# Placing VectorE work and tanh by a clock model at emission, dense item ahead of P·V, and an explicit order of dense items, in a fused attention and MLP kernel

## The chip, the cores and the metric

One NeuronCore of a Trainium2 chip. The metric is the device time of one execution in microseconds, on that core. Every time below is of a fast run; where two kernels are compared, the ratio is the mean time of one kernel's fast runs over the mean time of the other's fast runs of the same rounds, on the same chip, so it is not quite the ratio of the medians that are quoted beside it. The groups differ a little (the kernel before had medians of 1120.8 to 1123.9 us in the five groups of runs, two of them on one chip and two on another), so ratios are the numbers to compare across groups.

## The reference

`x` is 2048 tokens of 1024 features, bf16. The result is `x + attention(xn) * silu(mlp(xn))`, with 32 heads of 32 and an MLP width of 3584.

```python
xn = layernorm(x)
qkv = xn @ wqkv                                   # 32 heads, Dh = 32
p = softmax(q @ k.T * Dh**-0.5); s = (p @ v) @ wo
y = layernorm(xn)
h = gelu_tanh(y @ w1 + b1)                        # 2048 x 3584
g = silu(h @ w2 + b2)
out = x + s * g
```

## The kernel before

The program is emitted by Python into one instruction list per engine, with semaphores worked out from the tiles that each operation reads and writes. So the order of emission is the order in which each engine runs.

Attention is 512 *units*: 8 groups of 4 heads, 8 blocks of 256 queries, 8 blocks of 256 keys. In a unit PE computes scores S for four heads, row-tiled, into four PSUM banks; ACT does two exponentials of 128x1024; PE then does P·V and the row sums, column-tiled, into the one accumulator bank. PE is filled up with one *dense item* per unit, column-tiled, into the one remaining bank (bank 7): W1 (168 items), W2 (48 items cut into 3 or 4 parts), Q/K projections (84), V projections (48), the output projection WO (48). The tokens of the MLP go in six chunks, five of 352 and a last one of 288. Units 0 to 7 overlap the prologue (layer norm, first Q, K, V).

A finished dense item is evicted by VectorE. For W1 a chain follows on VectorE: add bias and evict, square, cube; then one tanh on ACT for two items; then two "gates" `(1+tanh)*x` on VectorE. After eight units VectorE also evicts the accumulator and scales it.

```python
def later(cost, fn, lag=1, first=False):          # queue a VectorE operation
    dq.append((cur["u"] + lag, cost, fn))         # not before unit u + lag
def run_dq(budget, limit=None): ...               # emit queued operations up to a budget in us

# W1, after its matmuls ...
def cube():
    op("vector", ...)
    if cubes[m2] == 2:
        act_tasks[cur["u"] + 1].append(tanh)      # tanh: in the next unit
def tanh():
    op("scalar", ... ACT.Tanh ...)
    for i, (xq, kq, fq) in enumerate(pairs[m2]):
        later(0.45, lambda ...: gate(i, xq, kq, fq), lag=0, first=soon)
...
while u < NU + 2 or ...:                          # the unit loop
    s_unit(u)                                     # PE: scores
    for t in act_tasks.pop(u, ()): t()            # ACT: tanh
    exp_unit(u)                                   # ACT: two exponentials
    if 2 <= u < NU + 2: pv_unit(u - 2)            # PE: P.V of two units ago
    for s in it.steps[lo:hi]: s(state["bank"])    # PE: dense item
    room = BUDGET - (0.8 if ended else 0.0)       # BUDGET = 1.35 us
    room -= run_dq(room)                          # VectorE: what is queued ...
    if hi == len(it.steps): it.finish(...)        # ... and then the eviction
```

The order of the dense items came from a loop with ratios and credits (W1 and projections mixed, then the W2 items of the chunk, and so on).

The softmax here doesn't subtract the row's maximum and nothing guards it: scores larger than these inputs give would overflow.

## Time and profile before

| | before |
|---|---|
| time, median of 3 | 1121.26 us (1120.38 to 1122.04) |
| span of the profiled run | 1120.0 us |
| first scores / unit 8 / last scores start at | 18.8 / 59.3 / 1098.9 us |

The page of the kernel before: the busy time of each engine with its share of the span, and the chain of work that ended last, followed backwards.

```profile
span 1120.0 us, 63277 instructions
...
PE 1085.4 (97%) x29952; PEld 692.4 (62%) x29952; DVE 621.5 (55%) x1415; ACT 1053.0 (94%) x1197; POOL 24.0 (2%) x64
...
PE 52%; ACT 43%; DVE 2%; DMA 1%; issue 1%; SPq 1%; DVEq 0%
ACT P L745 38%; PE ps L314 31%; PE ps L733 8%; PE ps L762 8%; PE ps L765 5%; ACT u L478 4%; DMA wq<-in_A_wqkv_dram 1%; DVE hT L484 1%; ACT thz L520 0%; PE ps L305 0%; SPq L223 0%; ACT xnT L308 0%; DMA xnT<-gT_scratch 0%; DVE xb L461 0%; DVE
```

PE is busy 97% of the time and ACT 94%, and the chain goes back and forth between them. Neither is simply "the" bottleneck, so the reading has to go to single units. This is the timeline of one unit with a Q item (columns: start us, duration us, engine, line, operation, out<-in, shapes, count, and in brackets the idle time of the engine before it with what ended it).

```profile
501.36 0.40 PE L733 MATMUL ps<-QT,KT 32*128 32x256 bf16 x8
...
501.69 0.29 PE L762 MATMUL ps<-P,VP 128*32 128x256 bf16 x4
...
502.14 1.37 PE L314 MATMUL ps<-xnT,wq 128*32 128x352 bf16 x32
...
503.44 0.40 PE L733 MATMUL ps<-QT,KT 32*128 32x256 bf16 x8
503.56 0.52 DVE L336 CAST QT<-ps 128x352 bf16<-128x352 f32 x1 [1.44 <-PE ps L314]
```

Read the starts, not the durations, since matmuls overlap: S to P·V 0.33 us, P·V to dense 0.45, dense to the next S 1.30. The Trainium skill, "TensorE: Matmul & The Clock Gate", section "Back-to-back issue gap", gives N/2.4 + 2.5 ns from one isolated matmul with N columns to the next. The trace agrees: 8 rounds of four column-tiled matmuls with N=352 are 8 x 149.2 = 1193 ns, and what is left of 1300 is about 107 ns for passing from column-tiled to row-tiled matmuls. S to P·V is 2 x 109.2 + 109 in the same way. So a W1 or Q unit takes PE 2.07 us when nothing disturbs it, a V unit 1.75. On ACT, exponentials start every 0.90 to 0.92 us, so a unit takes it about 1.83, and a W1 unit 0.34 more for its half of a tanh (0.68 us from the start of a tanh to the next start).

With these undisturbed times one can count *stalls* in the whole trace: for each stretch of S, P·V or dense matmuls, the time from its start to the start of the next, less rounds x (N/2.4 + 2.5) and less the passage (106 to 109 ns between S and the others, 10 between P·V and dense). I do this from unit 8 to unit 511. It gives 26.6 us for the kernel before: 15.2 ahead of S (PE waits for an exponential to free score banks), 6.4 ahead of a dense item (PE waits for VectorE to evict bank 7), and 5.1 as pauses *inside* runs of matmuls that wait for nothing.

What a stall ahead of a dense item looks like, in the timeline of the kernel before:

```profile
955.05 1.21 PE L314 MATMUL ps<-yTc,war 128*32 128x288 bf16 x32
...
956.19 0.40 PE L733 MATMUL ps<-QT,KT 32*128 32x256 bf16 x8
...
956.72 0.82 ACT L478 ACTIVATE u<-u 128x576 f32<-128x576 f32 x1
...
957.57 1.20 DVE L484 SCALAR_TENSOR_TENSOR hT<-u,xb 128x288 bf16<-128x288 f32 x3 [1.75 <-ACT u L478]
958.87 0.52 DVE L461 TENSOR_SCALAR xb<-ps,b1T 128x288 f32<-128x288 f32 x1
...
959.44 1.38 PE L314 MATMUL ps<-xnT,wq 128*32 128x352 bf16 x32 [2.30 <-DVE xb L461]
```

The W1 item that starts at 955.05 is done at about 956.3. Its eviction (L461) starts at 958.87 only: three gates (L484) stand ahead of it, and the first of them waited 1.75 us for a tanh (L478). PE is idle for 2.30 us before the next dense item. The waits by total time (who, for whom: us, times, longest) show that VectorE often stands like this, but charge PE little:

```profile
PEld ps L733 <- ACT P L745: 86.6, 260, 1.9
...
DVE gst L524 <- ACT thz L520: 32.1, 19, 2.2
...
DVE hT L484 <- ACT u L478: 13.5, 26, 1.7
PE ps L733 <- ACT P L745: 9.8, 29, 1.7
...
PEld ps L314 <- DVE xb L461: 4.7, 8, 2.6
...
PE ps L314 <- DVE xb L461: 2.7, 2, 2.3
```

The chain of waits in the stretch from 896 to 1000 us, which holds the last, 288-wide chunk. There a W1 unit takes PE only 1.86 us but ACT 1.83 + 0.29:

```profile
by line: ACT P L745 81.3%; ACT u L478 7.1%; issue 3.3%; PE ps L314 2.8%; DVE hT L484 1.2%; PE ps L733 1.1%; ACT thz L520 0.9%; SPq L413 0.9%; DVE xb L461 0.5%; DVE gst L524 0.5%; SPq L527 0.3%; PE ps L762 0.3%; PE ps L765 0.2%; DVEq L110 0.
```

89% of that stretch is ACT work on the chain (81.3, 7.1 and 0.9), so PE is the one that waits.

### The profile page before, as it was taken

The page shows a single profiled execution, that of the slowest core. Times are in us where ns is not written, and L with a number is a line of the kernel's source. Part 1 is how long each engine was busy: PE and PEld are TensorE (multiplying, and loading weights), DVE is VectorE, ACT ScalarE, POOL GpSimd, SP SyncE. Part 2 cuts the span into 40 slices and gives each one's busy share as a digit, 9 for nine tenths or more (in the row PEclk, how much of TensorE's full clock was granted, in tenths as well). Part 3 has the DMA queues.
Part 4 walks back from the last instruction along what each step waited for, and adds up shares of the span by engine and source line. Part 5 has one row for each costly group of instructions (what it writes and reads, how often), then busy time and mean ns, then how long its engine had stood idle before and what let it go on. Part 6 is the DMA issues. An engine that isn't in the chain of part 4 may idle for free.

```text
span 1120.0 us, 63277 instructions
## 1 busy us (share of the span) xinstructions
PE 1085.4 (97%) x29952; PEld 692.4 (62%) x29952; DVE 621.5 (55%) x1415; ACT 1053.0 (94%) x1197; POOL 24.0 (2%) x64
## 2 busy tenths in 40 slices
PE   6999999999999999999999999999999999899998
PEld 4856566666666666666656666666666666566666
DVE  7468862476642566842277642376742467424456
ACT  4899999999998999999999999999999999999993
POOL 4300000000000000000000000000000000000000
PEclk9999999999999999999999999999999999999999
DMA  9334465323354232233442245323244333477444
GB/s 236 69 115 154 135 143 156 110 78 107 95 150 138 85 102 84 78 89 97 145 126 82 79 126 144 100 79 107 79 122 138 107 107 97 138 175 161 89 104 116
DMA packets 202420, 129.93 MB, mean 116 GB/s; under 512 B 45488, under 2 KB 192944, under 8 KB 202160
## 3 DMA queue, kind: packets, MB, share of 16 engines
q1 hardware_dynamic: 197520, 125.86, 39.9%
q8 instruction: 234, 3.83, 1.4%
q0 software_dynamic: 4640, 0.02, 0.6%
q14 instruction: 26, 0.21, 0.1%
HBM read 104.87 MB, written 12.58 MB: 105 GB/s over the span
## 4 chain that ended last, share of the span: by engine, by line
PE 52%; ACT 43%; DVE 2%; DMA 1%; issue 1%; SPq 1%; DVEq 0%
ACT P L745 38%; PE ps L314 31%; PE ps L733 8%; PE ps L762 8%; PE ps L765 5%; ACT u L478 4%; DMA wq<-in_A_wqkv_dram 1%; DVE hT L484 1%; ACT thz L520 0%; PE ps L305 0%; SPq L223 0%; ACT xnT L308 0%; DMA xnT<-gT_scratch 0%; DVE xb L461 0%; DVE wq L567 0%
## 5 line engine op out<-in xcount | busy, mean ns | idle before, releaser
L745 ACT ACTIVATE P<-ps 128x1024 bf16<-128x1024 f32 x1024 | 972.4, 1067 | 29.1 <-PE ps L733 20.9
L762 PE MATMUL ps<-P,VP 128*32 128x256 bf16 x4096 | 262.2, 278 | 0.0
L765 PE MATMUL ps<-P,ones 128*32 128x256 bf16 x4096 | 257.2, 273 | 0.1
L314 PE MATMUL ps<-hT,war 128*32 128x352 bf16 (+1 forms) x5376 | 224.6, 308 | 0.5 <-issue 0.5
L314 PE MATMUL ps<-yTc,war 128*32 128x352 bf16 (+1 forms) x5376 | 224.1, 308 | 1.0 <-issue 0.7
L733 PE MATMUL ps<-QT,KT 32*128 32x256 bf16 x4096 | 203.6, 273 | 14.1 <-ACT P L745 9.8
L762 PEld LDWEIGHTS ps<-P,VP 128*32 128x32 bf16 x4096 | 107.5, 95 | 109.1 <-issue 102.5
L314 PEld LDWEIGHTS ps<-hT,war 128*32 128x32 bf16 x5376 | 141.7, 97 | 42.5 <-issue 1.2
L314 PEld LDWEIGHTS ps<-yTc,war 128*32 128x32 bf16 x5376 | 137.1, 97 | 47.7 <-DVE VP L350 1.4
L733 PEld LDWEIGHTS ps<-QT,KT 32*128 32x128 bf16 x4096 | 60.7, 92 | 159.5 <-ACT P L745 86.6
L461 DVE TENSOR_SCALAR xb<-ps,b1T 128x352 f32<-128x352 f32 (+1 forms) x168 | 96.1, 572 | 111.7 <-PE ps L314 111.1
L314 PE MATMUL ps<-xnT,wq 128*32 128x352 bf16 (+2 forms) x3200 | 129.7, 305 | 4.7 <-DVE xb L461 2.3
L516 DVE TENSOR_SCALAR zh<-ps,b2h 128x352 f32<-128x352 f32 (+1 forms) x48 | 27.5, 573 | 159.2 <-PE ps L314 159.0
L765 PEld LDWEIGHTS ps<-P,ones 128*32 128x32 bf16 x4096 | 109.4, 96 | 1.7 <-issue 0.4
L314 PEld LDWEIGHTS ps<-xnT,wq 128*32 128x32 bf16 x3200 | 81.7, 97 | 31.2 <-DVE xb L461 2.9
L484 DVE SCALAR_TENSOR_TENSOR hT<-u,xb 128x352 bf16<-128x352 f32 (+1 forms) x168 | 80.5, 507 | 14.0 <-ACT u L478 13.5
L467 DVE TENSOR_TENSOR u<-xb 128x352 f32<-128x352 f32 (+1 forms) x168 | 84.7, 504 | 2.4
L471 DVE SCALAR_TENSOR_TENSOR u<-u,xb 128x352 f32<-128x352 f32 (+1 forms) x168 | 84.0, 502 | 1.2
L478 ACT ACTIVATE u<-u 128x704 f32<-128x704 f32 (+1 forms) x84 | 68.0, 809 | 0.0
L314 PE MATMUL ps<-wq,xnT 128*32 128x256 bf16 x2048 | 66.3, 274 | 1.2 <-ACT xnT L308 0.6
L314 PE MATMUL ps<-xnT,OT 128*32 128x352 bf16 (+1 forms) x1536 | 62.4, 308 | 0.8 <-DVE wq L567 0.8
L776 DVE COPY accs<-ps 128x256 f32<-128x256 f32 x64 | 27.1, 424 | 60.5 <-PE ps L765 60.5
(44 smaller groups left out, 462.9 us busy)
## 6 DMA issues: line engine op xcount, KB each, us to landing
war<-in_B_w_dram SPq DMA_DIRECT2D x336, 256.0 KB, 4.0
wq<-in_A_wqkv_dram SPq DMA_DIRECT2D x12, 512.0 KB, 5.1
OT<-in_A_x_dram SPq DMA_DIRECT2D x16, 256.0 KB, 7.5
y_scratch<-OT SPq DMA_DIRECT2D x16, 256.0 KB, 2.7
xnT<-in_A_x_dram SPq DMA_DIRECT2D x16, 256.0 KB, 4.0
out_dram<-wq SPq DMA_DIRECT2D x16, 256.0 KB, 2.0
gT_scratch<-gst SPq DMA_DIRECT2D x40, 88.0 KB, 1.7
xnT<-in_A_wo_dram SPq DMA_DIRECT2D x1, 2048.0 KB, 9.5
```

What stands on the lines that cost most here:

```text
L314: ins = e.matmul(outs(j), lhsT=lhs(j), rhs=rhs, start=start, stop=stop, tile_position=(0, 32 * j), skip_group_check=True)
L461: op("vector", lambda e: e.tensor_scalar(xb[:, 0:n], bank(bk, 0, n), b1T[:, f:f + 1], None, op0=ALU.add), r=[("b", bk), "b1"], w=[kx])
L467: op("vector", lambda e: e.tensor_tensor(ub[:, 0:n], xb[:, 0:n], xb[:, 0:n], op=ALU.mult), r=[kx], w=[ku])
L471: op("vector", lambda e: e.scalar_tensor_tensor(ub[:, 0:n], ub[:, 0:n], 1.0 / 0.044715, xb[:, 0:n], op0=ALU.add, op1=ALU.mult), r=[kx, ku] ...
L478: op("scalar", lambda e: e.activation(ut[:, :, 0:n], ut[:, :, 0:n], ACT.Tanh, scale=0.7978845608028654 * 0.044715), r=kus, w=kus)
L484: op("vector", lambda e: e.scalar_tensor_tensor(hT[:, fq, 0:n], ut[:, i, 0:n], 1.0, xq[:, 0:n], op0=ALU.add, op1=ALU.mult), r=[kus[i], kq] ...
L516: op("vector", lambda e: e.tensor_scalar(zh[:, 0:n], bank(bk, 0, n), 0.25, b2h[:, nb:nb + 1], op0=ALU.mult, op1=ALU.add), r=[("b", bk), "b ...
L733: ins = e.matmul(bank(bks[j], kh * 256, (kh + 1) * 256), lhsT=KT[i2][32 * j:32 * j + 32, k0:k0 + 128], rhs=QT[i2][32 * j:32 * j + 32, qb * ...
L745: op("scalar", lambda e, p=p, sl=sl: e.activation(pb[:, 2 * p:2 * p + 2, :, :].rearrange("p a b q -> p (a b q)"), ps[:, sl * 1024:(sl + 1) ...
L762: e.matmul(bankq(ACC, j, 0, QW), lhsT=VP[vp][:, kb, vo + 32 * j:vo + 32 * j + 32], rhs=pb[:, j, kh, :], start=first, stop=False, tile_posi ...
L765: ins = e.matmul(bankq(ACC, j, QW, 2 * QW), lhsT=ones[:, 0:32], rhs=pb[:, j, kh, :], start=False, stop=last, tile_position=(0, 32 * j), sk ...
L776: op("vector", lambda e: e.tensor_copy(a[:], bank(ACC, 0, QW)), r=[("b", ACC)], w=[ka])
```

## The change

Intent: no arithmetic is changed; PE, ACT and VectorE should be kept from standing in each other's way. Three parts, which I call *placement*, *dense first* and *plan*:

- Placement: every operation is given a duration, and a clock per engine is kept while the program is emitted. A queued VectorE operation is emitted ahead of an eviction only if it will be done when the dense item is (100 ns of grace); a tanh goes ahead of the exponentials as soon as it delays them by at most 600 ns, or after three units.
- Dense first: in a unit the dense item goes ahead of P·V, and P·V lags one unit instead of two, with two P buffers instead of three.
- Plan: the order of the dense items is a written list, with W1 spread evenly among Q and V items and the W2 items cut into 2 to 5 parts.

```diff
+PLAN = """ a v a a a q a q a v ... w3 w4 w3 w4 v w4 w2 w2 w2 ... """   # cut
+    def clock(self, x, eng, dma, c, rdy): ...      # a clock per engine; c = modelled duration
+    def ready(self, eng, r=(), w=(), after=()): ...
+    LAG = 1; TOL = 100; ATOL = 600; AGE = 3
-        P = [... for i in range(3)]
+        P = [... for i in range(2)]
-        def run_dq(budget, limit=None): ...
+        def run_dq(until, limit=None):
+            while dq:
+                for i, (rank, _, ready, fn) in enumerate(dq):
+                    if limit is not None or max(pg.clk["vector"], ready) + 433.0 <= until:
+                        break
+                ...
             def fin(bk):                             # each eviction
+                run_dq(pg.ready("vector", r=[("b", bk)]) + TOL)
                 op("vector", ...)
-                        act_tasks[cur["u"] + 1].append(tanh)
+                        act_tasks.append((x.t + 60.0, tanh, 48 + 1.666 * n, cur["u"]))
+        def fill_act(u):
+            rdy = pg.ready("scalar", r=[...scores of unit u...])
+            while act_tasks:
+                r0, fn, cost, u0 = act_tasks[0]
+                t = max(pg.clk["scalar"], r0 + 40.0)
+                if t + cost - rdy <= ATOL or u - u0 >= AGE: act_tasks.pop(0); fn()
+                else: break
 # the unit loop
-            for t in act_tasks.pop(u, ()): t()
+            fill_act(u)
             exp_unit(u)
-            if 2 <= u < NU + 2: pv_unit(u - 2)
             ... dense item, its eviction ...
+            if NP <= u < NU + LAG: pv_unit(u - LAG)
+            run_dq(pg.clk["tensor"])
```

## The prediction

> **What bounds the kernel now.** The page's busy table has PE at 97% and ACT at 94% of 1120 us; the chain of waits alternates between them (PE 52%, ACT 43%). Attention runs as 512 units: scores S, P·V, one dense item on PE; two 128x1024 exponentials on ACT. The timeline (start to start of the first matmuls) gives a W1 or QK unit on PE as S 0.327, P·V 0.447, dense 1.300: 2.07 us. Other units: V 1.75, W2 parts 1.93 to 2.37. The Trainium skill ("TensorE: Matmul & The Clock Gate", section on the back-to-back gap) gives N/2.4+2.5 ns, 149 ns at N=352; the trace agrees: 8 rounds plus about 106 ns for changing between row- and column-tiled matmuls is 1.300. On ACT, exponentials start every 0.917 us, 1.83 per unit; a tanh pair adds about 0.66.
>
> Adding these undisturbed unit times over the trace: first S at 18.8 us, unit 8 at 59, then 504 units, then the 13 output-projection items left after attention and the final stores: about 1092 us. The other 28 us are PE stalls in the units. By stretches of the timeline: 8 to 10 us lie between units 416 and 464 (the last, 288-wide chunk, where W1 and W2 units are shorter on PE than exponentials plus tanh on ACT); about 3 us behind late residual/gate loads; about 1 us per 16 units in every W1 stretch, where a tanh falls badly or VectorE is late with an eviction; perhaps 5 to 7 us are gaps inside matmul runs put down to "issue", which no order of work explains.
>
> **What the change does.** No arithmetic goes away: same matmuls, 1024 exponentials, 84+48 tanh, the same VectorE operations. Two row/column switches per unit stay. Dense ahead of P·V lets P·V lag one unit instead of two; its exponentials should be done (P·V starts at least 1.3 us after S, the second exponential ends about 1 us after). By itself: no time. The gap in which the single dense bank is evicted stays P·V+S, 0.88 us.
> The gains must come from stalls: (a) VectorE operations are emitted so that none delays an eviction; the engine takes them in order (same page, spec table: strict FIFO), so emission order counts; that is worth 3 to 5 us. (b) tanh goes where its input is ready and it delays the exponentials least: 3 to 5. (c) The plan: summing unit times in blocks of 12, ACT's surplus over PE, which must stall PE, is about 17 us before and about 8 with the plan, of which 4.5 us is the last W1 chunk (28 narrow W1 items with only 11 QK items between): about 8 less; this overlaps (a) and (b). 38 instead of 35 projection items go inside attention; PE sums are unchanged, so nothing.
>
> Floor 1091, plus 8 surplus, 6 issue gaps, 2 others: **1107 us, range 1096 to 1115**. Faster by over 2%: 0.15; within 2%: 0.81; slower: 0.04.
>
> **What would show it.** PE, ACT and VectorE busy sums nearly unchanged; QK/W1 units' median still 2.07 us; PE's waits at S on the exponentials fall by half; dense items waiting for VectorE nearly vanish; the 416-480 stretch shortens by 5 us or more but ACT stays saturated there; the tail after the last exponential is about 3 us shorter, attention ends correspondingly less early; prologue unchanged.
>
> **What would make it wrong.** If P·V must wait for the second exponential, a stall per unit appears at P·V and the gain goes (slower). If the one-bank gap is overrun by VectorE (the model allows 100 ns), dense items wait in many units. If issue gaps are really waits that the new order removes, or the plan also absorbs them, it gets near 1097.

## The result, and the profile after

| | before | after |
|---|---|---|
| time, median (range), 4 runs each | 1120.82 us (1118.56 to 1122.04) | 1110.72 us (1110.16 to 1111.85) |
| ratio of fast runs, 95% interval | | 0.991 (0.9895 to 0.9925) |
| span of the profiled run | 1120.0 us | 1108.7 us |
| unit 8 starts / last scores start | 59.3 / 1098.9 us | 59.3 / 1090.7 us |
| from the last scores to the end | 21.1 us | 17.9 us |

The change takes 0.9% off: faster beyond doubt, well under 2%. The stalls, counted from the traces as above:

| units 8 to 511, us | ahead of S | ahead of dense | ahead of P·V | pauses inside runs | sum |
|---|---|---|---|---|---|
| before | 15.2 | 6.4 | -0.1 | 5.1 | 26.6 |
| after | 8.6 | 1.5 | 1.7 | 4.5 | 16.3 |

The difference, 10.3 us, is nearly all of the 11.3 us between the two spans; most of the rest is the shorter tail. Without its stalls the span after is 1108.7 - 16.3 = 1092.4 us, which checks the floor of 1091 in the prediction. Same page lines after:

```profile
span 1108.7 us, 63340 instructions
...
PE 1082.7 (98%) x29952; PEld 706.5 (64%) x29952; DVE 630.4 (57%) x1415; ACT 1049.5 (95%) x1197; POOL 24.0 (2%) x64
...
PE 65%; ACT 32%; DVE 2%; issue 1%; DMA 0%; POOL 0%
PE ps L366 41%; ACT P L773 29%; PE ps L761 10%; PE ps L790 7%; PE ps L793 7%; ACT u L524 3%; DVE stats L303 1%; PE ps L357 1%; ACT thz L566 0%; DMA OT<-in_A_x_dram 0%; DVE hT L335 0%; DVE wq L614 0%; POOL lnp L313 0%; DVE mv L305 0%; DVE xb
```

Busy sums hardly moved (PE 1085.4 to 1082.7, ACT 1053.0 to 1049.5, DVE 621.5 to 630.4); the chain now runs through PE for 65% instead of 52%. A unit after the change, with a tanh and a gate in it:

```profile
300.60 0.40 PE L761 MATMUL ps<-QT,KT 32*128 32x256 bf16 x8
300.75 0.83 ACT L524 ACTIVATE u<-u 128x704 f32<-128x704 f32 x1
...
300.93 1.38 PE L366 MATMUL ps<-xnT,wq 128*32 128x352 bf16 x32
...
301.61 0.53 DVE L530 SCALAR_TENSOR_TENSOR hT<-u,xb 128x352 bf16<-128x352 f32 x1 [0.73 <-ACT u L524]
...
302.13 0.28 PE L790 MATMUL ps<-P,VP 128*32 128x256 bf16 x4
...
302.36 0.53 DVE L389 CAST QT<-ps 128x352 bf16<-128x352 f32 x1 [0.23 <-PE ps L366]
...
302.68 0.40 PE L761 MATMUL ps<-QT,KT 32*128 32x256 bf16 x8
```

The unit still takes 2.08 us from S to S. The gate (L530) again waits for its tanh (0.73 us), but only one gate is ahead of the eviction (L389), it ends at 302.14, and the eviction starts as soon as the dense item is done. The waits after:

```profile
DVE hT L530 <- ACT u L524: 62.2, 68, 3.1
PEld ps L761 <- ACT P L773: 53.9, 204, 1.9
...
PEld ps L366 <- DVE xb L507: 33.8, 158, 0.3
...
DVE gst L570 <- ACT thz L566: 25.5, 36, 1.4
...
PE ps L761 <- ACT P L773: 5.5, 14, 1.7
...
PE ps L366 <- DVE wq L614: 0.2, 1, 0.2
```

VectorE waits for tanh far longer than before (62 us for gates instead of 13.5), and it costs PE little: the only wait of PE's dense matmuls for VectorE that is left is the last line, 0.2 us, and that of the scores for the exponentials fell from 9.8 to 5.5. A gate may still wait ahead of an eviction, but in the unit above it was done before the eviction's data was there. One line can mislead: weight loads wait 33.8 us "for DVE xb". That is 158 times about 0.21 us, the ordinary passage from S to a dense item, which was put down to "issue" in the kernel before and now happens to follow an eviction. It is no stall. And the same stretch of the chain:

```profile
by line: ACT P L773 47.7%; PE ps L366 28.0%; PE ps L761 8.2%; PE ps L790 5.0%; PE ps L793 4.9%; ACT u L524 4.9%; issue 2.0%; ACT thz L566 0.3%
```

ACT's part of the chain is down from 89% to 53%, not to zero.

### The profile page after: what moved, and what is told of

It reads as the page before. It is cut to its first block, busy times and chain, and to the rows that moved or that the text cites. A ratio compares the mean times of both kernels' runs of the same rounds, so it can differ in the third digit from the quotient of the medians.

```text
span 1108.7 us, 63340 instructions
## 1 busy us (share of the span) xinstructions
PE 1082.7 (98%) x29952; PEld 706.5 (64%) x29952; DVE 630.4 (57%) x1415; ACT 1049.5 (95%) x1197; POOL 24.0 (2%) x64
## 4 chain that ended last, share of the span: by engine, by line
PE 65%; ACT 32%; DVE 2%; issue 1%; DMA 0%; POOL 0%
PE ps L366 41%; ACT P L773 29%; PE ps L761 10%; PE ps L790 7%; PE ps L793 7%; ACT u L524 3%; DVE stats L303 1%; PE ps L357 1%; ACT thz L566 0%; DMA OT<-in_A_x_dram 0%; DVE hT L335 0%; DVE wq L614 0%; POOL lnp L313 0%; DVE mv L305 0%; DVE xb L507 0%
## 5 line engine op out<-in xcount | busy, mean ns | idle before, releaser
L790 PE MATMUL ps<-P,VP 128*32 128x256 bf16 x4096 | 257.5, 273 | 0.0
L366 PE MATMUL ps<-yTc,war 128*32 128x352 bf16 (+1 forms) x5376 | 226.4, 309 | 0.4 <-issue 0.4
L366 PEld LDWEIGHTS ps<-hT,war 128*32 128x32 bf16 x5376 | 128.0, 96 | 76.2 <-issue 27.6
L366 PEld LDWEIGHTS ps<-yTc,war 128*32 128x32 bf16 x5376 | 127.5, 96 | 75.8 <-DVE xb L507 17.2
L790 PEld LDWEIGHTS ps<-P,VP 128*32 128x32 bf16 x4096 | 110.4, 97 | 21.4 <-issue 1.7
L530 DVE SCALAR_TENSOR_TENSOR hT<-u,xb 128x352 bf16<-128x352 f32 (+1 forms) x168 | 83.8, 508 | 62.3 <-ACT u L524 62.2
L366 PEld LDWEIGHTS ps<-xnT,wq 128*32 128x32 bf16 x3200 | 77.5, 97 | 41.6 <-DVE xb L507 10.7
L513 DVE TENSOR_TENSOR u<-xb 128x352 f32<-128x352 f32 (+1 forms) x168 | 82.5, 508 | 0.8
L366 PEld LDWEIGHTS ps<-wq,xnT 128*32 128x32 bf16 x2048 | 50.2, 96 | 14.0 <-DVE xb L507 5.5
```

Of the source, the lines that this page charges most:

```text
L366: ins = e.matmul(outs(j), lhsT=lhs(j), rhs=rhs, start=start, stop=stop, tile_position=(0, 32 * j), skip_group_check=True)
L513: x = op("vector", lambda e: e.tensor_tensor(ub[:, 0:n], xb[:, 0:n], xb[:, 0:n], op=ALU.mult), r=[kx], w=[ku], c=151 + 1.042 * n)
L530: op("vector", lambda e: e.scalar_tensor_tensor(hT[:, fq, 0:n], ut[:, i, 0:n], 1.0, xq[:, 0:n], op0=ALU.add, op1=ALU.mult), r=[kus[i], kq] ...
L790: e.matmul(bankq(ACC, j, 0, QW), lhsT=VP[vp][:, kb, vo + 32 * j:vo + 32 * j + 32], rhs=pb[:, j, kh, :], start=first, stop=False, tile_posi ...
```

## The experiments

The three parts can be switched one by one. With all three undone, the emitted instruction order on each engine should equal that of the kernel before, so I take "before" as the corner of the cube without any part. Theory A, the one of my prediction: the gain is the sum of stalls removed by placement and plan, and dense first is worth nothing by itself. Rivals: B, placement carries all; C, dense first carries it; D, the plan carries all. All results here are correct unless said otherwise; each kernel was timed in five rounds. "Excess" of some units is their whole time over the undisturbed one, whatever the cause.

A word on noise. The traces show what a mean granted clock below 1 is here: in the run of "placement alone" with 0.998, one stretch of 3.4 us inside the units has a clock of 0.50; in the run of "plan alone" with 0.995, two stretches of 3.4 and 6.8 us. Such a stretch takes about half its length, 1.7 us for 3.4 us, from a busy PE. Most runs of the kernel before in these groups have one by their clocks, its profiled run of the main comparison has none. "Clock-corrected" below means that 1.7 us is taken off for each such stretch that a run's clock (0.998 or less) implies. This is an estimate, and it assumes that the main comparison had none in any run.

### Plan alone

```diff
 # the kernel before
-        mlp = []; ... ratio, credit ...      # order by ratios
+        for tok in PLAN.split(): ...         # order by the list
```

> The kernel before with only the new order of dense items; P.V ahead of dense, VectorE queue and tanh as before. Theory A (the stalls of PE go, and part of them is a matter of which items stand side by side): 1113 to 1116 us, the waits of PE at S for the exponentials fall by 4 us or more, those at the dense item for VectorE stay near 6 us. Rival B (placement carries all): 1119 to 1122 us. Rival C (dense ahead of P.V carries it): 1119 to 1122.

Measured: 1119.89 us, ratio 0.9976 (0.9951 to 1.0001). Stalls ahead of dense 5.8 us, as expected; those ahead of S 18.3 us, not fewer (3.3 us of them lie in the two half-clock stretches of this run, which leaves about what the kernel before has). Theory A's number was wrong: the plan alone gives about 2.7 us, not clear of zero. B and C named the right range here.

### Placement alone

```diff
 # the changed kernel with the old order of items, and
-    LAG = 1
+    LAG = 2                                  # P.V ahead of dense, three P buffers
```

> The kernel before with only the new placement of VectorE work and tanh; old order of items, P.V ahead of dense. Theory A: 1113 to 1116 us, the waits of PE at the dense item for VectorE fall from 6 to about 2 us, the waits at S by 2 to 4. Rival B: 1110 to 1112. Rival C: 1119 to 1122.

Measured: 1119.31 us, ratio 0.9964 (0.9946 to 0.9983), 4.0 us. Stalls ahead of dense fell to 2.0 us as expected; those ahead of S stayed at 15.5. So neither A's 1113 to 1116 nor B's 1110 to 1112 came. The 4 us are about what the dense stalls lost (4.4 us).

### Dense first alone

```diff
 # the kernel before
-            if 2 <= u < NU + 2: pv_unit(u - 2)
             ... dense item, run_dq(room), eviction ...
+            if NP <= u < NU + 1: pv_unit(u - 1)
```

> The kernel before with only the dense item ahead of P.V (lag of one unit, two P buffers). Theory A: 1119 to 1123 us, nothing gained, perhaps 1 to 2 us of new waits at P.V. Rival C (the reordering is itself the gain): 1113 or less.

Measured: 1133.53 us, ratio 1.0085 (1.0061 to 1.0109): 9.5 us *slower*. Both expectations missed. The stalls ahead of dense rose from 6.4 to 20.5 us; P·V waits were 2.2 us, about as expected. The timeline of one of them:

```profile
296.33 1.38 PE L366 MATMUL ps<-yTc,war 128*32 128x352 bf16 x32
296.73 0.82 ACT L530 ACTIVATE u<-u 128x704 f32<-128x704 f32 x1
...
297.53 0.28 PE L813 MATMUL ps<-P,VP 128*32 128x256 bf16 x4
...
297.57 1.40 DVE L536 SCALAR_TENSOR_TENSOR hT<-u,xb 128x352 bf16<-128x352 f32 x3 [1.38 <-ACT u L530]
...
298.88 0.58 DVE L513 TENSOR_SCALAR xb<-ps,b1T 128x352 f32<-128x352 f32 x1
...
299.52 1.38 PE L366 MATMUL ps<-xnT,wq 128*32 128x352 bf16 x32 [0.62 <-DVE xb L513]
```

The W1 item of 296.33 is done at about 297.7. But three gates (L536) are queued ahead of its eviction (L513), and they could not start before the tanh of the same unit (L530) had ended, at about 297.5. So the eviction comes at 298.88 only, and the next dense item is 0.62 us late. With P·V ahead of dense, the dense item ends 0.45 us later in the unit, and the same gates hold its eviction up less.

The Trainium skill, "TensorE: Matmul & The Clock Gate", section "Architectural detail: the array is 16× 32×32, not 1× 128×128", says of ACT and VectorE that their queues are strict FIFO. The traces agree: here the eviction's data was there for over 1 us and the gates went first; and in the stall shown from the kernel before, the data was there at about 956.3, VectorE stood idle until 957.57 for the gate at the head, and the eviction was not taken in that time.

### Gates a unit later, in the kernel of the last run

```diff
-    later(0.45, lambda ...: gate(i, xq, kq, fq), lag=0, first=soon)
+    later(0.45, lambda ...: gate(i, xq, kq, fq), lag=1, first=soon)
-    later(0.45, last, lag=0)
+    later(0.45, last, lag=1)
```

> The kernel of run dense_first_only with one thing changed: the gate, the VectorE operation that reads what tanh wrote, and its like after W2 are queued one unit later, so not in the same unit just ahead of the eviction. If the 14 us of new waits at the dense item there come from gates that wait for tanh at the head of VectorE's queue, the waits fall from 20 to 8 us or less and the time from 1133 to 1118 to 1124 us. If it is the earlier end of the dense item as such (less time for the queue), they stay above 14 us and the time above 1129.

Measured: 1123.26 us, ratio 0.9999 (0.9987 to 1.0011), against 1.0085 without this edit; stalls ahead of dense 7.9 us instead of 20.5, both as expected if the gates are the cause. In the waits, those of PE for the eviction of a W1 item went from the first of these lines to the second (each from its own run):

```profile
PE ps L366 <- DVE xb L513: 10.1, 21, 2.9
```

```profile
PE ps L366 <- DVE xb L513: 2.9, 9, 0.4
```

So the loss was the gates that wait at the head of the queue, not the earlier end of the dense item. Two numbers changed in the old queue buy back what dense first had cost.

### The changed kernel with P·V first again

```diff
-    LAG = 1
+    LAG = 2
-        P = [... for i in range(2)]
+        P = [... for i in range(3)]
```

and `pv_unit` ahead of the dense item.

> The changed kernel with P.V put back ahead of the dense item (lag of two units, three P buffers); plan and placement new. Theory A: 1108 to 1111 us, no slower than the changed kernel, and without its 1.7 us of waits at P.V. Rival C: 1116 or more.

Measured: 1113.44 us, ratio 0.991 (0.989 to 0.9931), the same ratio as the whole change. Stalls at P·V 0.2 us, as expected. In absolute time it lies above the range, in a group where the kernel before too was 2.7 us slower. Rival C falls: once VectorE's queue is placed, dense first neither gains nor loses a time that these intervals, ±2 us, can show (clock-corrected this kernel is at 0.992). It does move stalls: this profile has 13.5 us ahead of S (1.2 of them in a half-clock stretch), where the change has 8.6, and fewer at P·V. Dense first frees one P buffer.

### The changed kernel with the old order of items

```diff
-        for tok in PLAN.split(): ...
+        mlp = []; ... ratio, credit ...
```

> The changed kernel with the order of dense items of before. Theory A: 1113 to 1116 us, the units from 416 to 480 lose about as much as in the kernel before. Rival B (placement carries all): 1110 to 1112.

Measured: 1121.22 us, ratio 0.9976 (0.9961 to 0.9991). Rival B falls. The excess in units 416 to 479 is 13.1 us, against 13.9 before and 8.6 after, as expected. The time is worse than I expected: without the plan the other two parts are worth 2.7 us together. Not all of that is the order of work: this profile has 9.1 us of pauses inside runs against 4.8 in the change (gaps of over 0.25 us), which is 4 of the 8 us between the two sums of stalls.

### The changed kernel with old placement, old queue, old tanh

Three kernels: VectorE queue *and* tanh by budgets and unit numbers again; only the queue; only tanh.

```diff
 # queue
-                run_dq(pg.ready("vector", r=[("b", bk)]) + TOL)      # ahead of each eviction
+                    room = BUDGET - (0.8 if ended else 0.0); room -= run_dq(room)
 # tanh
-            fill_act(u)
+            for t in act_tasks.pop(u, ()): t()
```

> The changed kernel with VectorE queue and tanh placed as before, by budgets and unit numbers. Theory A: 1114 to 1117 us, the waits of PE at the dense item back at 5 us or more. Rival B: 1119 or more. Rival D (the plan carries all): 1110 to 1112.

> The changed kernel with only the VectorE queue by budgets again; tanh still placed by the model. Theory A: 1113 to 1116 us, waits at the dense item 4 us or more. If VectorE's order is worth nothing: 1110 to 1112.

> The changed kernel with only tanh placed by unit number again; VectorE queue by the model. Theory A: 1112 to 1115 us, waits at S up by 2 to 4 us. If the place of tanh is worth nothing: 1110 to 1112.

Measured: old placement 1132.05 us, ratio 1.0069 (1.0049 to 1.0089), stalls ahead of dense 17.8 us. Old queue 1127.69 us, 1.0032 (1.0014 to 1.0049), stalls ahead of dense 16.1. Old tanh 1115.52 us, 0.9924 (0.9909 to 0.994), stalls ahead of S 12.7 instead of 8.6. The range for the old placement was missed (B's was met, but B had fallen by then), as was that for the old queue: in the changed kernel VectorE's queue is worth some 14 us, because it also pays for dense first. Rival D falls. The place of tanh is worth 1.6 us by the ratios (0.9924 less 0.991, of two groups of runs, intervals overlapping); its absolute time lay 0.5 us above the expected range. But that is the low reading. Every run of "old tanh" had a clock of 1.000 and most runs of the kernel before did not: clock-corrected it is 0.994, or 3.8 us. And within one group, old placement less old queue, which differ in the place of tanh alone, gives 4.1 us (±2.4; mean times 1131.7 and 1127.6). The 4.1 us more of stalls ahead of S fit that.

### No tanh in the last chunk

Wrong result. (The check does not see errors of this size.)

```diff
-    op("scalar", ... activation(ut[:, :, 0:n], ut[:, :, 0:n], ACT.Tanh, ...))
+    op("scalar", ... activation(ut[:, :, 0:na], ...))      # na = 8 in the last chunk, else n
```

> The changed kernel, result wrong on purpose: in the last, 288-wide chunk the tanh of W1 covers 8 columns instead of 288. If ScalarE's surplus binds PE there, as the sums say (4.5 us), units 416 to 463 lose 3 us less or more, and the time is 1105 to 1108 us. If the stalls there have another cause: 1109 to 1112.

Measured: 1108.8 us, ratio 0.987 (0.9853 to 0.9887); against 0.991 that is 4.5 us, the size of ACT's surplus in the sums of the prediction, but only 3.9 clock-corrected and 1.9 by the two medians. The absolute time is just above the range, in a group where the kernel before was 2.6 us slower. Stalls ahead of S in units 416 to 463 went from 3.4 to 0.2 us. The chain from 896 to 1000 us:

```profile
by line: PE ps L366 55.9%; PE ps L763 15.6%; PE ps L795 10.6%; PE ps L792 10.2%; ACT P L775 4.5%; issue 3.8%; ACT thz L568 0.3%
```

ACT is down to 5% of it. (The whole excess of those units fell by 1.2 us only, less than the 3 I had named, because this profile has 4.6 us of pauses inside runs there against 2.2.) So what PE still waits for at S in that stretch after the change is ACT's tanh work: that is shown. Its size is some 2 to 4.5 us, and that no other order of the items could remove it was not tested.

### Weights loaded once

Wrong result on purpose: later chunks use whatever weights are in the buffers.

```diff
             c, k = divmod(g, 11)
+            if c > 0: return
```

> The changed kernel, result wrong on purpose: the W1 and W2 pieces are loaded for the first chunk of tokens only, later chunks use what is there. If the 4 to 6 us of pauses inside runs of matmuls come from the instruction fetch being held up by the other DMA traffic, they nearly vanish and the time falls to 1105 to 1108 us. If the fetch is late for another reason, they stay at 4 us or more and the time at 1109 to 1112.

Measured: 1106.34 us, ratio 0.9851 (0.9836 to 0.9865), 6.6 us under the ratio of the change (5.5 clock-corrected, 4.4 by the medians). The time is in the range expected if the loads delay the instruction fetch; the pauses were halved and did not nearly vanish. One pause as the changed kernel has it, in a W2 part with 28 matmuls, from its timeline:

```profile
964.71 0.40 PE L761 MATMUL ps<-QT,KT 32*128 32x256 bf16 x8
...
965.03 1.04 PE L366 MATMUL ps<-hT,war 128*32 128x288 bf16 x27
...
967.49 0.30 PE L366 MATMUL ps<-hT,war 128*32 128x288 bf16 x1 [1.41 <-issue]
```

27 matmuls, then 1.41 us of nothing, then the last one of the same round of four: no semaphore stands there. Pauses of over 0.4 us of this kind, anywhere in the span, sum to 5.5 us in the kernel before, 5.5 after and 2.8 here, and after 120 us only one of 1.0 us is left here, while the changed kernel has five with 4.6 us. The trace's packet records show what they have in common. The instructions come in packets of their own:

```profile
q8 instruction: 234, 3.83, 1.4%
```

These are 234 packets of 16384 bytes, that is 256 instructions of 64 bytes each, if I take the packets to be PE's: 234 x 256 = 59904, exactly the 29952 matmuls and 29952 weight loads. In the two kernels, before and after, all 12 pauses end 2.2 to 2.7 us after the start of such a packet. After the first 60 us, two packets start 4.5 to 4.6 us apart in the median; distances up to 8.0 us occur with the loads and none above 6.9 without. The packet ahead of a pause is a late one: in the ten pauses after 60 us it starts 4.7 to 8.0 us after the packet before it, in eight of them over 6.4. And the block size shows in the trace: the last two pauses of the kernel before, at 1018.9 and 1025.1 us, stop PE after 54635 and 54891 matmuls and weight loads, exactly 256 apart. The Trainium skill, "Runtime: NRT & Kernel Launch", section "Instruction fetch mechanics", describes just such refills in blocks of 256 instructions and calls their cost "mostly hidden". In this kernel mostly, but not wholly. That other DMA traffic is what delays them is supported by this run; the whole gain is not only pauses, since the stalls ahead of dense and P·V also fell, by 2.1 us together.

### Weight loads paced

```diff
-    op("sync", ... dma_start(dst, src), w=[("war", s, q)], ...)
+    op("sync", ... dma_start(dst, src), w=[("war", s, q)], ..., after=pg.lists["tensor"][-1:])
-                sp_tasks[cur["u"] + i].append((load_sub, g, q))
+                sp_tasks[cur["u"] + i // 2].append((load_sub, g, q))
```

> The changed kernel with the W1 and W2 loads paced: each 256 KB piece also waits for the scores of its own unit, two pieces in a unit, so that they no longer start as a burst as soon as the buffer comes free. If bursts of loads hold up the instruction fetch, the pauses inside runs of matmuls (5.5 us in the changed kernel, 2.8 with the later loads removed) fall to 3.5 us or less and the time to 1106 to 1110 us at the earlier chip's level, a ratio to the kernel before of 0.987 to 0.990. If pacing does not matter or new waits for late weights eat the gain: 0.991 or more.

Measured: 1110.57 us, ratio 0.9879 (0.9862 to 0.9896). Pauses 1.8 us, and the stretch from unit 8 to the last scores is 1028.1 us instead of 1031.5. Is it a better kernel? Not settled. The ratio is inside the range, but the median is that of the change (1110.72), and the kernel before ran at a clock of 0.997 to 0.998 in that group while this one ran at 0.999 to 1.000, which alone could be worth 2 us. Its profile also started 3.3 us late, waiting for the first QKV weights. And the sum of pauses varies between kernels that load alike, from 2.8 to 9.5 us. No version clearly beat the changed kernel with correct results.

### All ratios to the kernel before

| plan | P·V first, old placement | P·V first, new placement | dense first, old placement | dense first, new placement |
|---|---|---|---|---|
| old | 1 | 0.9964 | 1.0085 | 0.9976 |
| new | 0.9976 | 0.991 | 1.0069 | 0.991 (the change) |

Each entry has an interval of about ±0.2%. 0.001 is 1.1 us.

## Why the prediction was right, point by point

The time was right: 1107 with a range of 1096 to 1115, and 1110.72 came; and within 2% was the likeliest class. Of the 14 us that 1107 meant, 10.1 came. The sum of stalls was forecast by the right causes, but part of it is luck: the worth of dense first, and how the parts depend on each other, were not seen.

- *What bounds it.* Right. The floor of 1091 plus stalls holds: stalls fell from 26.6 to 16.3 us, and I had put down 28 and 16 (8 surplus, 6 issue gaps, 2 others). The median W1 and Q unit is 2.07 us before and after.
- *What would show it.* Stalls at S fell from 15.2 to 8.6 us, by 43%, near the half that was said. Those at dense went from 6.4 to 1.5. Units 416 to 479 lost 5.3 us of excess, and ACT is still the larger part of the chain there. The tail is 3.2 us shorter: by the trace 37 instead of 35 projection items start ahead of the last scores (two more, not three), and one P·V fewer comes after them. Unit 8 starts at 59.3 us in both.
- *Dense ahead of P·V "by itself: no time".* Wrong as put, by 9.5 us. I had looked only at PE and the exponentials, and had asked whether the gap for the eviction stays 0.88 us. It does, but it begins 0.45 us earlier in the unit while the gates still wait for the same tanh. The statement holds only with the new queue, where P·V first and dense first have the same ratio. The total came right because the change brings both together, which the prediction did not give as a reason.
- *(a) VectorE's queue, 3 to 5 us.* Right for placement alone with the old order: 4.0 us, stalls at dense 6.4 to 2.0. In the changed kernel it is some 14 us, since without it dense first loses.
- *(b) tanh, 3 to 5 us.* Within noise of right with the new order of items: 1.6 us by the ratios, 3.8 clock-corrected, 4.1 within one group with the old queue. With the old order it is not visible in the stalls at S (15.5 against 15.2).
- *(c) The plan, about 8 us, overlapping the others.* 6.0 to 7.4 us with the new placement, 1.8 to 2.7 without it. Placement and plan together give 10.1 us where they give 4.0 and 2.7 apart. I had expected them to overlap; they don't. That they help each other is not shown: the 3.4 us between 10.1 and 6.7 have an interval of about ±3.2, and clock-corrected only 1.2 is left. In the traces, too, what the plan gains with the new placement is in good part pauses inside runs (6.7 us in "placement alone", 3.2 with the plan added, 5.5 in "plan alone", 4.9 in the kernel before), and with one trace each this may be chance. One may argue that evenly spread tanh work only helps when tanh can take the place that the even plan makes for it; no run isolates that.
- *ACT's surplus in the last W1 chunk, 4.5 us.* Shown as a cause by the run without that tanh; its size is less sure: 3.2 us of stalls at S, 4.5 us by the ratios, 1.9 by the medians.
- *Issue gaps, 5 to 7 us, which no order of work explains.* Right in kind (5.5 us in both traces); by all signs they are late instruction fetches, and fewer when the weight loads go.

## What to carry to other kernels

When two engines are each some 94% busy or more, count the stalls ahead of each kind of work against undisturbed start-to-start times, and expect a reordering to gain at most about that sum in the stretch that was counted. On an in-order engine, an operation that waits for another engine must not stand ahead of one that frees a buffer; here that one rule was worth 10 us in the kernel with dense first alone, and moving work earlier on PE without it had lost as much. Test parts of a change together as well as alone: dense first cost 9.5 us or nothing, depending on the queue. And before two ratios are compared to 2 us, look at the clocks of both groups: one half-clock stretch of 3.4 us is worth 1.7.

## What the Trainium skill lacked or had wrong

- "TensorE: Matmul & The Clock Gate" (section "Back-to-back issue gap") calls N/2.4 + 2.5 ns the isolated gap, and says that it over-counts in a sustained stream at large N. In this stream of column-tiled rounds of four it holds at N=352 to within 1 ns (149), and at N=256 (109). The two row-tiled rounds of a unit's scores start 120 ns apart at N=256. No run here has N=512, where the page's example lies.
- "TensorEngine Tiling (Array Packing)" (section "Key Properties") says that changing the tiling mode drains TensorE, but gives no cost. These traces fit it: a passage between row-tiled and column-tiled matmuls takes 106 to 109 ns (counted as above, with the 11 ns inside the scores), one between P·V and dense, both column-tiled, 10 ns. With two passages a unit that is about 0.21 x 512 = 110 us of this kernel's 1120. That draining is the reason is not shown.
- "Runtime: NRT & Kernel Launch" (section "Instruction fetch mechanics") has the 256-instruction refills right but not what a late one costs: pauses of 0.4 to 1.9 us, 5.5 us in all, ending 2.2 to 2.7 us after the packet starts, and half gone (2.8 us; after 120 us 1.0 instead of 4.6) when 73 MB of the 126 MB of other traffic are taken away.
